# A new order of operations for a two-layer linear-attention and GLU kernel, searched with longer and more frequent delays of DMA transposes

The kernel runs on one core of one Trainium2 chip. The metric is the device time of one execution in microseconds (us), median over runs.

## The reference

Two layers, applied in turn twice (A, B, A, B) with the same weights, on x of shape (1, 2048, 512) in bf16.

```python
def _A_ref(x, wqkv, w_phi, wo):                  # 32 heads of 16
    q, k, v = ...                                # x @ wqkv, split
    pq = jnp.einsum("bhsd,hdf->bhsf", q, w_phi)
    pk = jnp.einsum("bhsd,hdf->bhsf", k, w_phi)
    phi_q = concatenate([softmax(pq), softmax(-pq)])     # phi_k likewise
    kv = jnp.einsum("bhsf,bhsd->bhfd", phi_k, v)
    z  = jnp.einsum("bhsf->bhf", phi_k)
    o = einsum(phi_q, kv) / (einsum(phi_q, z) + 1e-6)
    return o.reshape(B, S, D) @ wo

def _B_ref(x, W_gate, W_up, W_down):             # F = 1376
    return (relu(x @ W_gate) * (x @ W_up)) @ W_down

x = A_x
x = x + _A_ref(_layernorm(x), ...)
x = x + _B_ref(_layernorm(x), ...)
x = x + _A_ref(_layernorm(x), ...)
x = x + _B_ref(_layernorm(x), ...)
```

## The kernel before

The kernel records 2114 operations, each with its engine, its planned duration and what it reads and writes. A list scheduler then simulates the engines and takes, whenever an engine comes free, the ready operation of the highest priority. The priorities are a table of 2114 numbers (`RANKS`, packed as text), found by a search outside the kernel; `MOVED` lists operations that run on their second engine. After that each engine gets its own fixed stream with semaphore waits.

```python
    def schedule(self, rounds=12, ranks=None, moved=()):
        for i in moved:
            o = self.ops[i]
            o.eng, o.fn, o.ii, o.lat = o.alt
        self.links()
        if ranks is not None:
            self.boost = {}
            return self.forward([float(r) for r in ranks])
        # ... (priorities from the graph, if there is no table)

    def emit(self, e, eng, sems, dsems):
        for o in self.seq[e]:
            for s, c in o.waits:
                if isinstance(s, tuple):
                    eng.wait_ge(dsems[s[1]], 16 * c)
                else:
                    eng.wait_ge(sems[s], c)
            ins = o.fn(eng)
            # ... (the semaphore increment)
```

A token tile is 128 rows of x, and there are 16. The layer norm's result y of a tile is transposed before PE multiplies with it. Most tiles are transposed by a DMA that the SP engine issues (a few by PE itself); so are the q features, the attention output o and the remainder of the GLU's hidden values. That makes 99 DMA transposes, of 128 KB each for y.

```python
            if (l, t) in PE_Y:
                # ... PE transposes y into PSUM (line 655), ACT copies it out
            else:
                op("sp", lambda e, yt=yt, dst=dst, c=c:
                       e.dma_start_transpose(dst.ap()[:, :, c:c + 128], yt.ap()),
                   reads=[yr], writes=[rr], dma="tr", nbytes=500, name=f"yT{l}.{t}")   # line 660
# ...
        for b in range(2):
            op("sp", ... e.dma_start_transpose(...), dma="tr", name=f"qT{l}.{t}.{b}")     # line 767
# ...
            op("sp", lambda e: e.dma_start_transpose(oT_.ap(), ot_.ap()),
               reads=or_, writes=[oTr], dma="tr", nbytes=500, name=f"oT{l}.{t}")          # line 931
```

Names in the text: "yT of tile 13, layer 2" is the transpose of y of token tile 13 in the second A layer (the four layers are numbered 0 to 3). Lines: L587 and L606 fold w_phi into the weights at the start; L682 computes the K and Q features, L739 V, L754 Q in another layout, L786 the key-value sums, L837 and L901 the attention output, L936 the product with wo, L966 gate and up, L994 the GLU remainder, L1020 down; L646 is y, L655 a transpose of y on PE.

The softmax here doesn't subtract the row's maximum and nothing guards it: scores larger than these inputs give would overflow.

## Time and profile before

| | before |
|---|---|
| time, median of 3 runs | 385.53 us (385.19 to 386.15) |
| profiled run: span | 383.0 us |
| PE busy in it | 371.3 us, 97% |
| PE's idle time in it | 11.7 us |
| DMA transposes | 99, of which 18 landed 3.0 us or more after issue, the others 2.4 to 2.8 |

The busy row says that PE is the bound; the stretches say where it idles at all; PE's wait list says what for. The prediction below shows these views, line by line. A landing is the moment at which the data of a DMA are there, and "DMA to landing" counts from the issue.

### The profile page before, as it was taken

Reading aid. Unit: us, or ns where it says so; the run is one execution under the profiler, and the core shown is the slowest. Engines: PE = TensorE matmul, PEld = TensorE weight load, DVE = VectorE, ACT = ScalarE, POOL = GpSimd, SP = SyncE. Lnnn points to the kernel's source line nnn. Section 1 sums busy time; section 2 is a strip of 40 time slices with the busy share of each in tenths; the row PEclk is TensorE's granted clock in tenths of the full one; section 3 lists DMA queues with packets and bytes.
Section 4 is the critical chain, followed back from the end, with each engine's and each line's share of the span. In section 5 each row is a group of like instructions: output and inputs, shape, how many; then the busy total and the mean of one; then the engine's idle time right before and its main releaser. Section 6 shows DMA issues by size and latency. Waiting matters only on the chain.

```text
span 383.0 us, 6646 instructions
## 1 busy us (share of the span) xinstructions
PE 371.3 (97%) x2429; PEld 206.4 (54%) x2471; DVE 292.0 (76%) x646; ACT 199.7 (52%) x618; POOL 58.2 (15%) x123
## 2 busy tenths in 40 slices
...
DMA packets 64944, 23.94 MB, mean 63 GB/s; under 512 B 56112, under 2 KB 64656, under 8 KB 64912
## 3 DMA queue, kind: packets, MB, share of 16 engines
...
## 4 chain that ended last, share of the span: by engine, by line
PE 80%; DVE 10%; DMA 4%; ACT 2%; issue 2%; POOL 1%; SPq 0%
PE pb L966 36%; PE pb L1020 18%; PE pb L936 7%; PE pb L754 4%; PE pb L739 4%; PE pb L837 3%; PE pb L994 3%; DVE z L701 2%; DVE phik L708 2%; PE pb L1022 2%; PE pb L786 2%; DMA yT<-y 2%; PE pb L682 2%; DVE z L703 1%; DVE y L646 1%
## 5 line engine op out<-in xcount | busy, mean ns | idle before, releaser
L974 DVE TENSOR_TENSOR expq<-gate,pb 128x512 bf16<-128x512 bf16 (+1 forms) x100 | 57.1, 577 | 46.6 <-PE pb L966 46.3
L973 ACT ACTIVATE gate<-pb 128x512 bf16<-128x512 f32 (+1 forms) x100 | 50.8, 510 | 68.9 <-PE pb L966 64.7
L966 PE MATMUL pb<-yT,Wu 128*128 128x512 bf16 (+1 forms) x396 | 82.8, 336 | 0.3
L966 PE MATMUL pb<-yT,Wg 128*128 128x512 bf16 (+1 forms) x393 | 81.4, 336 | 0.4
L1020 PE MATMUL pb<-Wd,expq 128*128 128x512 bf16 (+2 forms) x320 | 75.4, 373 | 0.5
L966 PEld LDWEIGHTS pb<-yT,Wg 128*128 128x128 bf16 x400 | 38.3, 98 | 30.1 <-DMA yT<-y 0.4
L966 PEld LDWEIGHTS pb<-yT,Wu 128*128 128x128 bf16 x400 | 38.8, 98 | 28.9
L1020 PEld LDWEIGHTS pb<-Wd,expq 128*128 128x128 bf16 x330 | 31.6, 98 | 35.4 <-DVE expq L974 0.6
L620 DVE BATCH_NORM_STATS2 stats<-x_sb 128x6 f32<-128x512 bf16 x64 | 43.4, 686 | 1.0 <-DMA x_sb<-in_A_x_dram 0.5
L695 ACT ACTIVATE phik<-pb 128x512 bf16<-128x512 f32 x72 | 39.6, 639 | 1.2 <-PE pb L682 1.2
L1028 DVE TENSOR_TENSOR x_sb<-x_sb,pb 128x512 bf16<-128x512 bf16 (+2 forms) x33 | 21.9, 665 | 20.3 <-PE pb L1022 20.0
L629 ACT ACTIVATE lnv<-mv,eps 128x1 f32<-128x1 f32 (+1 forms) x58 | 16.8, 297 | 35.3 <-DVE mv L621 34.8
L700 POOL TENSOR_TENSOR t<-phik 128x512 f32<-128x512 bf16 x16 | 19.1, 1195 | 88.3 <-ACT phik L695 83.2
L758 ACT ACTIVATE expq<-pb 128x512 bf16<-128x512 f32 x56 | 30.7, 604 | 3.1 <-PE pb L754 2.9
L739 PE MATMUL pb<-wv,yT 128*128 128x512 bf16 x123 | 30.0, 380 | 1.6 <-DMA yT<-y 1.2
L936 PE MATMUL pb<-wo,oT 128*128 128x512 bf16 x120 | 30.9, 379 | 0.5
L874 DVE TENSOR_TENSOR t<-pb,sm 128x384 bf16<-128x384 f32 x56 | 29.4, 547 | 1.5 <-POOL sm L864 1.5
L682 PE MATMUL pb<-Wkp,yT 128*128 128x512 bf16 x124 | 29.6, 379 | 0.1
L646 DVE TENSOR_SCALAR y<-x_sb,mv,rstd 128x512 bf16<-128x512 bf16 x63 | 27.1, 439 | 2.3 <-ACT rstd L631 1.8
L851 ACT ACTIVATE sm<-pb 128x48 f32<-128x48 f32 (+1 forms) x84 | 14.4, 211 | 26.5 <-PE pb L837 26.4
L754 PE MATMUL pb<-yT,Wqp 128*128 128x512 bf16 x106 | 25.9, 380 | 0.4
L939 DVE TENSOR_TENSOR x_sb<-x_sb,pb 128x512 bf16<-128x512 bf16 x32 | 21.8, 683 | 3.4 <-PE pb L936 3.1
...
## 6 DMA issues: line engine op xcount, KB each, us to landing
...
yT<-y SPq DMA_TRANSPOSE x55, 2.5
...
```

The costliest lines, as they stand in the source:

```text
L620: op("dve", lambda e, t=t: e.bn_stats(stats[:, t, :], x_sb[:, t, :]), reads=[res("x", t)], writes=[res("st", t)], ii=600, lat=690, name=f" ...
L646: yop[l, t] = op("dve", lambda e, t=t, yt=yt: e.tensor_scalar(yt.ap(), x_sb[:, t, :], mv[:, t, 0:1], rstd[:, t, :], ALU.subtract, ALU.mult ...
L682: i = e.matmul(kt.ap(), src.ap()[:, ic, c0:c0 + 128], W[:, ic, :], start=(ic == 0), stop=(ic == 3))
L695: op("act", lambda e, s=s: e.activation(ft.ap()[:, :, s, :], kt.ap().rearrange("p (g f) -> p g f", f=64), ACT.Exp, scale=(1.0, -1.0)[s]), ...
L739: i = e.matmul(vt.ap(), src.ap()[:, ic, c0:c0 + 128], wv[:, ic, :], start=(ic == 0), stop=(ic == 3))
L754: i = e.matmul(qt.ap(), Wqp[:, ic, c * 128:(c + 1) * 128], src.ap()[:, ic, :], start=(ic == 0), stop=(ic == 3))
L758: op("act", lambda e, g=g: e.activation(es[g][0].ap(), qt.ap(), ACT.Exp, scale=(1.0, -1.0)[g]), reads=[qr], writes=[es[g][1]], ii=477, lat ...
L936: i = e.matmul(wt.ap(), oT_.ap()[:, c, :], wo[:, c, :], start=(c == 0), stop=(c == 3))
L966: i = e.matmul(pt.ap()[:, 0:n], W[:, ic, fc * 128:(fc + 1) * 128], src.ap()[:, ic, a * 128:b * 128], start=(ic == 0), stop=(ic == 3))
L973: op("act", lambda e: e.activation(st_.ap()[:, 0:n], gt.ap()[:, 0:n], ACT.Relu), reads=[gr], writes=[sr], ii=110 + n * .72, lat=230 + n * ...
L974: op("dve", lambda e: e.tensor_tensor(ht.ap()[:, a * 128:b * 128], st_.ap()[:, 0:n], ut.ap()[:, 0:n], ALU.mult), reads=[sr, ur], writes=[h ...
L1020: i = e.matmul(pt.ap()[:, 0:n1 - n0], hT[l, s, fc].ap()[:, c:c + 128], Wd[:, fc, n0:n1], start=(fc == 0), stop=False)
```

## The change

The search that found `RANKS` and `MOVED` draws noise on the durations of operations and prefers orders that stay fast under it. The new tables come from a search in which a DMA transpose was delayed more often and for longer. Code and operations are the same; the diff has only tables.

```diff
 RANKS = (
-    '9sqX)M*%<xF9<gXe*!)T-Uk8*!T_EG5eDW1I|w}pRs}x@*9O=J`~-LhNe46t1PB8NDhRIwB?t-#D+i(m$p;Sr$_HEr0ssL3Q3n733;;X`I|dE_0|2cB9S9!?',
     ... (all 45 lines of the table replaced)
+    'hX*1D^at(*Lk0~9^#{!dK?q$0vIVgRqz9=76bKLqAO#=>p9kLuzy~l09SE8S3J44cF9_=f90&yn>jioQF$kan82~;A7YH8!EC?e2HwYF80RRO6001)xApjNt',
 )
 MOVED = (
-    73, 75, 93, 101, 143, 245, 305, 325, 471, 472, 475, 481, 497, 547, 599, 627, 643, 644, 647, 651, 667, 692, 699, 715, 716, 740, 767, 771, 788, 791,
-    812, 1470, 1488, 1536, 1544, 1561, 1568, 1592, 1612, 1640, 1656, 1657, 1680, 1681, 1688, 1705, 1712, 1729, 1732, 1736, 1752, 1760, 1780, 1800,
+    73, 79, 87, 93, 101, 143, 245, 325, 471, 472, 475, 481, 490, 497, 498, 547, 579, 599, 620, 623, 627, 643, 644, 647, 651, 667, 675, 699, 716, 723,
+    739, 743, 747, 764, 812, 819, 835, 836, 839, 1470, 1536, 1537, 1544, 1568, 1592, 1609, 1616, 1633, 1636, 1640, 1656, 1684, 1688, 1705, 1708, 1712,
+    1732, 1736, 1756, 1760, 1777, 1801, 1804,
 )
```

More of the change, by code (lines that the diff above doesn't have):

```diff
@@ L1110 @@
 RANKS = (
-    '9sqX)M*%<xF9<gXe*!)T-Uk8*!T_EG5eDW1I|w}pRs}x@*9O=J`~-LhNe46t1PB8NDhRIwB?t-#D+i(m$p;Sr$_HEr0ssL3Q3n733;;X`I|dE_0|2cB9S9!?',
-    '7623g1ppTa1OSQ#90(Br3IMhRBM77bD+VM8%>|+X6#yIr2mqG_r3YFD4FD4W69|C^e+OIw2>>AoY5?g55eO{^4hUla1_9v%1^^}q5&+c%6bL>CTmUl&3jnbP',
-    '8VDi?3<#eGga=s$c>#z9;0Im?3kZ=1!~tdi76?rT^aVZ!IS4HSK?M~E5(w)D^anu*ya750L<a~6@dNS)HV7~X#Rs_uRR?te2LKreum|S{qzCQ?dk41%H3#Vj',
-    'A_Wf!vIpA-#|9z?p$0ApLI+a^DhJO8^9P0pm<I_6)CV94tq0Nv2ME0e`Ub)W1_=5GCkLAc&<9ip9taZ$kO#d7MF+D7{Ri9z1_#Cml?Q4ET?eKId<Sp`Xa)oa',
@@ L1115 @@
-    'x(CAs7zecm5(kb4@dkYd8V7s^<p%%<+y@{B&IZ2*uLnE@;RoFZ1_kB>UI(rRP6F=(F$muWWC!9083$DbwgPGfX9xBNTLxeT)dwsH*9Gqe=mo?FZU@u`ZwEIA',
-    '^#*VTF$ehu5CAm>8UQ&5z6PfUSqG~IT?PRL{st%q<OGHWHwCr_pazl#%?2d~U<c0w?geHCD+v1qV+XDVjt1uj?*$$QO9%S~2?rMk8wZmH9|zC{GY9bnH3<I(',
-    '*apl8G6<grqy|R@K?igOhX-Z`7X~;7BL|`fTL+#7>jtj|s0Tj>S_hd1$p-WWxCS-{atDA1P6q=AiwCC$wg$omQU{I&yasg!-UeR>CI^uQf(P~m<Ofj(xdw#>',
-    '%?BL^VF!-}NCyK3rUvl`od=2sGzTvS(+B7Vng&1z>IPW_+XfW}mIn|Ai3f`YL<Xz}!3MVmb_Wp$YX*!5o(Ba66bGCI$_9i6(FWuOAqU<C(guYGKn17<#0HN9',
@@ L1119 @@
-    '`~`ak8wP&{ng<O8>IJL?{RWW*vIY_cQw5a<N(b5ofdxGVJO+9OB?n&yMFtNAqXlvWj|Wc&*#m$C<^}`=^#|<+PX_!3p$FIl{RBJ&kpTz-f&{$-s{_;n+XHR|',
-    'tpsfav<6`YivzI%;|Ie7Uj@Ge-vc`Wa|OExTn5<(MhEx?zz2*3$Oh;K@CR21bO#6qa|Y%IzXt#adIdcNBL+AK!3QY_@&+gf{0Bn@_XpVqDF!VEss%#@{|B50',
-    'm<4MGg9n!eVg_Xd3j(SF90#oiCIuS^*aSxhPzUb^@dN<~5C!lBg#~y8d<16%Xa#x)Z3evr?E~utaRyxl;|6C2$po1NB?bEj)doxltN<qnItQf&aR=H5G6(Dj',
-    'qX(%61qg`-k_U|issySA%mzdS3I}KhkOmkC)(7|pxCi+M%Lo1k?FXv|&IhmtHwF+04G6;rc?MPoJO`ZyP6Z1FYzF-UPzI9+I|pnB-v-DB_695mn+6RAz6S>f',
@@ L1123 @@
-    '4F_Qa&IF(ba|8wk@&(ofy9Uz*1qXEpeg^>ut_9Ht;RXx_5(WMR_Xa2iX$O=C2nP%Ymk0R;CI<fn+67kxsRn!nF$D_+LkAuPas)63_5>XURRl~1%LWAnQ3bRI',
-    'hzE@a*9QUycLm%9)dkE1Z3is|-35UI5d|0q#|Hog@CG^ta|iAQeFiZGsRWG%6b8ly&<3Cd8U>*RN(EyD*#tTRW(1Z6+Xd$Z2L{*$wFhqo?gVEAR0e|vp9LBQ',
-    'HU?M+!v!P;-UN~bFa@s#SO(4oegqr^umrmW83qmpvjpY^4+ixGCj}J-zXgy5hy{BEhXttxG6uW_F$84>s|6tiYXs~BV+5N8QU$;U#Rbs?j0PqIlLYq!KL*VN',
-    '<pjb7hX#xVQv|vNw*_Mc9|oiZP6R3jZU$flUIlOk7X?WLxCH0~WCcY8@B^X*Zv+4ZWd~dZNd!Ixx&(Lx9tBth_XDW{IRj<|6a<zAtpno)N(RydAqEWveFTsM',
@@ L1127 @@
-    'lm^QM2?cisGX*OJ4+p&kIt9Q5MFWNf-vz@2B?P<#1O?Ou69lXTQUn<Vas%!I&jiW@)&%ebbOizjRtDt;5Ck0s!UVDfSp+WyY6N8kvjN-$wgf5!eg((`=mHu9',
-    'iUcDBVFgwMxdk}{;01vMTLdfwg9BOwPz09*LIxxS9|AH3%L6L}Tm)$ZrvyR-0|l4{vj(69?Ezi{5(FX!-2_(!s07;tN(3wh3<Z@1{RM&s(giRENCr6uY6Zy!',
-    'F9z%e?FF0$&jzdpyaz`Gcm@^+ss}v>3I=utc?T{Ax(4?J>Id@$1O|ZyQwEs_I0h#MMFmL)(+1rJ4hIVd$OWDSrUgL;Pz6W@#{@11<puZ!l?0Ooq6K6I(*!dH',
-    'P6kT`HUxwO`UMsS!37%yKn5HJT?8!!lm+4imIF)$qXrNL8UxG)vjxQlDFv_vng#y^I|R!FwFR98IR*Oz69v}<gavj5#{;tiLjr6AGXy^aa{~zkYXkZMxdX-o',
@@ L1131 @@
-    'bpwI}RRbOaUjt(U+yYz!>;(x1j|Hs)H3ilNBnKb_>I0tx{{v(L6$G#XbOXo&ZUU|YQU=`vI|FV6DFhb-`~xflxdKK7WCWZ8E&~??9Rzs=g9J?kq65wYy8|}^',
-    'Z3I{ZD+4nFssWe-G6A~)xC6BUlL3eVHUgXi9|27T1q8|iz6In3O9f2^djvHEpaXvcQUfXjO#|HmPy-SJsRJAXbOM$F(f}3%6a{tydjiD(qy@wUeg=XCPX#mu',
-    'm;_=4GzRGe3I*8(iUk7%jRcDYI|Z}^TLp3kfCkhA69%ybYXy1)e*}XCLIrsQBm|`e?F2>!rUWPjfCYaA^91h%uLN)e$_3{H2nFi|b_ARRE(9n9^#sKPJp*t9',
-    '=>?|+k^_DN(F17%0t5vE<N}HVg91wg>jU5fF9g~Go&);=kON)=nFBrpQv>V+00Zm-T?1JI1_Uq!_5=9@AO$!CR|eq(=mU8J*8?~MNdx@?%>p3<Bm;{Cg#_dS',
@@ L1135 @@
-    '4+J9vZv(CbngsF!)&q?L9|QFQPXm+#AOi*i?E;bnQ3QPju>_d}i3Onq;0Cw_KLvCI2L*8j&jkkrR0Z<}u?A@dbp@ye3j|sP^aJ|@76jo19|evCRR-Gvxdh_`',
-    'w*<xo!2}Eh;s$60s{|he#R3im-vkx~_yi{e5d_r(Ed<~Lh69NMz5-|iG6YHk3IoytM*~y>O9ABq5CfY8;{(kDbp+l6Oa!h1Z3CzSrUQ%v`~tuOcLPHM*8(L2',
-    '!~*yO+5@`;0t1=@{sXrHK?4~Bw*v?RvICO?S_4@E3<C`VNCO@O;saL$#RED7d;|IeR0CTB?gH-tq5@$9LIdXl;R0X-Yz34AP6KHLG6T#5n**N&ECsX$#|4%I',
-    'AO_F`)&j%?hy=O=cmqcS0tNI0qXbU`0R+<m2?PEFi3EoPAp{!)L<EZh&jKn1z68tyU<7dlA_PVRJ_Nu7vIO}983Yal(gWoKqXRz#+ymzWl>?OmKm$Aj*a9L0',
@@ L1139 @@
-    'gaTUv1Ow{=;sWyn(*r{U7zBm{X9IWwH3N|Y>H@z4lL8n64g(znu>(c}Jp{Z1E(O8^zXM+cL<0*0y#mGp`UF4%CIjFB8Ul<0{{kig$OE+lv;*J*Vgzmj$pR4r',
-    'O9M6o!veMgHU-K8Gz6Ce!2;?8)dIu=7zNG(kp!y(x&qMzBL&_8;sm__y8<)<4gr|}Isg{{o&gyEApoQSdI5m|6ajYudIFsR0|Ivkd;!V;Dgn&^Py+Y>uL95m',
-    '=>rM`2n1#Wk^(>kdjSCjZ34gn@&o_`z5`SQhy!m00|SBr8~_6W_5fA`odkpcgaMrc;{Xi;fdU=^umhz8JpoJuz5yu*Vh3pf@B&8wNCFuFK>|nw_yTeQ;{x*n',
-    '?*fSe8vrB##sdTb7y#`6Z~^ZCLIDQ?wFImKp#vZQY6IQ^fB{_sI0Z=oH3C)udjtLfhXZT`p#mNO;{hlE=>ib}G6FdQD*|2uI0B~w#sKgE(E{!OGy@m`d;+}z',
@@ L1143 @@
-    't^pweCjof^u>vpxYXIi~Q3I<1Q38zt76H@(AOUFtL;>yrfC32ug#vK^eFD`0g#)w#j|15Psss4~Y65oxiUKhMO#+qyD*;#l$N(t;Pyx3AR{~!EWdZ^LUjn5A',
-    '&;X7D%>my6gabDO@&oAs4g%x>LIM{8b_1^fqysPm6a#AlRs!V!fCE+mj{@2RC<2rMaRbW&W&$Sz@d4%nEdufZHv(D!J^|4Hp8}fz;sL?}69V}GQv$dGVFH^1',
-    'xB&nHmjVX^&jGOj6ao_iyaE;i*a1uerveuN$pD%GS^~KN{{j920s`v+{Q;i=YyvX?JOEMvumRrzaRMCzY5}hS&H--#A_8Lpn*s9xvI2|%`T=MF^Z}p&>;a|$',
-    'rT_{7dIL=WZvuJ%DFQ44&;tAb^8vL1_yKzW3jvA%4*}!=(g7v`#{n<_5CYKwNC5@{MgV^SYXLg|OaWd13<C85g#k+fhXOAHKLSAkR{>K2f&n)G$^k(Dm;!zR',
@@ L1147 @@
-    'F#$gT2LWIKZ2^M;kpR~LRRIM8SOPZzWdZa8=m5h2#{wt-Q~^2xPXRyyGXZ@8jsd9vN&z7OoB<~Qask!=qXN$WF9B}>lmK7=QvfLdSpXUVtpO?kqXD!5Jp!iy',
-    'tN|MXDFed+mH<)#r2*9e906MaVF6|V4FPom^Z-f#wgHC$0Re6R@Bl~vE&)yewgB+}HUXRfmjGt~Yyf@%KmbDkzyOE<m;lEBWdJPzVE`onX98ma!2>=53Id7&',
-    '`v9{7@d82s<^e$jWdi{N9{{WZqyiNMQUZ<wjRG|Q5CK&Jzye<ZN&-&;VgmO9R{%2tM*_(ME&?S2BLY|hi2)G;kOHOxMFJH9+yO-ZIsz&J4+Gi(VgO(Q^#kew',
-    'AOcAOkpeLSeFNwLJOV8N83OwOodVMVq5#wZ`~kuNh5-@+Z~|}uh5(2G7y^p{cmcWrXaY|F-2uh{y8){JX#gk#&;cX@Cj$2Yp#iu6h630Ck^tZUo&XX7{Q!6X',
@@ L1151 @@
-    'jsWEWVguU&sR5M%-T*`b90GF!LjgYkr2_T=nE`GAlmXcRi2&IEngUn>`T(Z^T>(u2a{(&=XaSi5_5v>g6$4}faRF=r0RqVZMFC;~H39bkP65*Z4+81{umDB@',
-    'v;YVJxd4X%Gy$#vmjROivH(N?bOBxgBmuVoI{{q)b^*)*wE&C(asVs=O8}?>;Q{La+yFQMkO7?l1OdMRo&q!gfdT&jz5r1HfB+o<A^~&&bpV(Fr~obiG5}ct',
-    'r2wq}qX60f>;RAeBLUU{paS^-WC7OzTmg#!PyjvvTL3Wt)BwK#OaK)D9RS||jR1oHg#fw$H~`B4IRKRaBLFr4vj8RlZ2(jN+W?>d%K_&AB?0~b$N@$IvH=?c',
-    'k^u|>p#a4J;Q&zpe*l62j{z(IX93~>!2$IE%m6$AS^=5>!2o^$@&LR5!~g&R=>VSqssITAr~!5WRRD7U69MJ`-2gcONdSBRcK~Dn8v%I$JpeBN&H#@9A^-&e',
@@ L1155 @@
-    'eE={3',
+    'hX*1D^at(*Lk0~9^#{!dK?q$0vIVgRqz9=76bKLqAO#=>p9kLuzy~l09SE8S3J44cF9_=f90&yn>jioQF$kan82~;A7YH8!EC?e2HwYF80RRO6001)xApjNt',
+    '5da1N4geDX7XTapA^;TtKnVW^5C8%I1OPt>+XZU^B>*G{2>=NM2LLz-3jhNE5(qX2CkO)wJqQ^H4FK^68VD)~9sv6X8vq;uG6>fN!2$395&$9y6aXLy%mEk(',
+    'JP4Nu8Ue@$+Xw6h4*)I(`3BnrGzi27WdsfguLm9o1PC1fiUwu}1_&|)@CP9X7yzpWyamYzs0Z=|tOgnYP6kp3Z3i?5<_C@k2?&)1Q3q)Ug$H5>>j%sR)&}hd',
+    '=La7L7zg|Z$pZ)oHwT*s_y^?$GzJj}?gsz}NC$BSkO##F0to&Grw4ooO$8eWeFuIAMh653k_S)+2MA;bYX{&5o(4S!bO%-k=?1(8eg<|2ItO_N3I@{$xCej+',
@@ new lines @@
+    'i3idLTL<q4BnN^9We4X5QwKf=#s>-q$OcUZy#~$%<p&rA)(7?nUj`Betq0==X$2(+lLr0-mIk*6ssxk<DF`bFZ~`d+fdy3tBM96FzXwYO6$i8j3IKKnya%@i',
+    '90#HX3kabGI|xz*oCZJ!nFmA#^ac+IoCh@qItU#BkObERA_bKP_62+e3<XsL2mnO|3;^K=&j*MHCI}!0?gjw|rUp3&JO?KS@C6VDF9*2?U<cs_+6GhwLkEEd',
+    'ItDlg7YDlsDhA#K{RKP)T?ftuGX~oRMh4slK?aZprv{M+zXnGKum>Rr2?tdNatD|P&<3Rk69;<-Fb9_g0|(^>I0eE7p9bRvK?hL-ZwK=RB?iC-u?5Zss0J$r',
+    'MF+tK00+?qg9i@>U<GamI|tbYH3!!Ro(C!iG6!Y`83(}!Q3i(wP6tc}od=x;cLvx8%LaV~#|AD3iwCd<X9w~I`~`9b{RUnI-v%QFN(R>kKnDW`nFdJ))Cb)I',
@@ new lines @@
+    'cLZq$-vvho-353B{|Ed8V+LRbbp`hYBLuPp_y$%5Y6c7ktOqCrfdu9Q=LNO|$p*&*vIlAb7Xp?8YXjc{tOQ5}kOeaYbOBNT2?Fc~-2!d_EC2)p?gUu{d;p#V',
+    'D+dGyXa*++djRqW0SLwen*@^p3Iw?UdIo_9vj(*X)d%(lH3*0XVF!f-u?A-bn+8?}_Xj@&wg-&|{s!~~<OVqi)ds=_R0oC!ods71-Um?yGyseS*$3(d`Ul+y',
+    'V+S7yz6Q((dI!P;z6Bu$d<K69k_Hn9M*uAaYzG|#Y6pb|=mx0<z6aw14F`7zln0Lolm(>$t_4H~$OT>oeE}N>>I0((kp@x*lLzPrlmx>B9tSoCB?TV^76*L>',
+    'rU$hKcn4Ys=?4}DSqDr8IR*m-m<Id?C<T@WjRva*+6VmyfCm%@J_9uXh6N)BaR(>|p$BjWTm+2;qXk?CbOuZWIsmW%{{>zLga<ta>IWSL$_5e#MFxxn0s^`Q',
@@ new lines @@
+    'm<7QF#Rba;%?1Sqd;~fL%LUd2pa(k!SOZT7EC)6S^9Q{L;s>q=VFAhq`3Lm|wg%A$LI*nqumt-BWCSn;y9CMvvj^Y?iv}D9<Oc=^83t$vNeAHtSO;?i(go%Q',
+    'kp*i8a0aIZpasAM83pD9pac^I{{$8VJp>d6hy*MKa|c-l&<AV=l?I9jZ3MUmga)Vug9fPuLIjQlc?K&5c?E|9ngu2Y5(N$hCj~(T#|H@p!UdNF`32Mlx(9;=',
+    'J_Zj48wSAxeFRViVFbDbqz2Xm9t7D1y#>DoDFyEZx&-$InFWjm9tL&-;|2x>e+GI5^aQm9xCAl=Km_6jv;_$T=L6FQh6Zp2K?7F?2L&1jKLvLMjs!debOp}@',
+    'R|Wk9umv&&VFuy_B?qMiDF;Rcl>}o2-3A>6R|7ExZUi(1rvv^4>ICNmc?6FJmIOEiUj&H-83Zl`o&_=kfCTje*#YSSjRQ*svIhDFQv+KD4FnMeWCl(I!~_)v',
@@ new lines @@
+    'qXxqUZ3W;300aUBss;K5mjwI*f&%~s?FQup@&a20eFJ3%rvhaKXa(E_h67*(RRx>{gawfV7Y20(hXn@*I0p9wbq9$C{sZ;|#{{PY%L8f!%>t|g6b1JKe*~BW',
+    'j{_+Kp9B*GL<S}V8w1w^j0Xq=UIEkqS_5_jzXaq1*amY3O$3Pqf&~f#vjnOG8w3~z0|OQWUIR}AT?GvT(*+y_g9O3@t^)!FKL<|*(FMZ?HU;1WQwHw_-Ujdn',
+    '=>>uZOaNR3@dk?pNd&qAF$NU~UkB*~2L>nzJq2zCE(oy%N(WB{xdt}|ss~*L3<k{w#0Sm?0tYP!%LIf3qy=^b&jxJ<Aq5KsGY1+5n+0M9Zw40y*aZy+Rs*;N',
+    '=mq8lBn2n~$pwxEiUg|zBnDar4g|CYWCc714h0SeR0cu@m;(z2IR#h-$OKLWg#~H^VgnNfq6JU}(gw-}tp?r%!v!z~IRuacS_LWvCI!0#?gRY;LjxrQp#zx#',
@@ new lines @@
+    '8Uj894+NV7QUllnWda5S#|3)@(*#}w8U<MdxdmSZt^{=h+6DRp69W|kXamLqNCb)lo&vxG;RGWE2nCq~VFSJbF#;?FH3aGfZv>JA+ysjRq6C@)g9Et)wFA`x',
+    '#05_RGy^yTKm&gRLI73(&H^F>gaVWT#R232hX6AL)dQpihy~9Ay#u=j1O(^<g#$(e<OK%<>jU2cZv*%Qj01lHssc6yMgZLb*Z~Uy_5!c~Yz2}7p8_`pYy@Ei',
+    'r3Ntv3kMws0R}Y%Tm~ux1qa3kuLDa23I%2b2nU%2Zw0mmiUlGDKL&CI)C5TdSOo+HVg-o<%mvv5Qw0wLF9rYwQUo;vss=3wTLd=*9|nd59|Y<FCI&VGw*(~v',
+    'odlo;bOSj9W&^(iX#<=B4g(Mak^(~n;RC}1(gUIg)dh0}wgSKdegkj>Faz}hlLhAj`vUR=F$4z$5eKXV&;{TFp#=K`?*n`T4+R1Q?E)SJMF4sOCIk5bX$0H@',
```

21 lines of the change are left out of this document (added).

## The prediction

> **What bounds the kernel now.** I read first the page's busy row and 40 slices, then the stretches of time, then PE's own wait list, then PE's timeline around each wait, and last the landing times of the DMA transposes.
>
> The page:
>
> ```profile
> PE 371.3 (97%) x2429; PEld 206.4 (54%) x2471; DVE 292.0 (76%) x646; ACT 199.7 (52%) x618; POOL 58.2 (15%) x123
> ...
> PE 80%; DVE 10%; DMA 4%; ACT 2%; issue 2%; POOL 1%; SPq 0%
> ```
>
> PE is busy 97% and holds 80% of the chain that ended last. The change reorders work and moves none to or from PE, so it can win at most what PE idles: 383.0 - 371.3 = 11.7 us. Of that, 20.00 - 17.58 = 2.4 us lies in the first 20 us and 43.00 - 40.43 = 2.6 us in the last 43 (nearly all in the last store). The stretches, whose columns are window, length, and busy time of PE, PEld, DVE, ACT and POOL:
>
> ```profile
> 0.00:20.00 20.00, 17.58 (x149) 12.53 (x152) 17.65 (x61) 15.88 (x41) 7.19 (x33) 1.00 0.62 192
> 20.00:40.00 20.00, 19.86 (x94) 9.03 (x95) 19.80 (x38) 19.57 (x59) 13.79 (x18) 1.00 0.55 120
> ...
> 128.00:200.00 72.00, 71.68 (x354) 33.95 (x358) 46.21 (x99) 23.46 (x67) 2.06 (x4) 1.00 0.16 31
> 200.00:215.00 15.00, 13.67 (x62) 6.07 (x63) 15.00 (x21) 13.82 (x37) 1.16 (x1) 1.00 0.40 78
> ...
> 340.00:383.00 43.00, 40.43 (x205) 19.59 (x207) 16.84 (x27) 6.63 (x12) 0.00 (x0) 1.00 0.13 40
> ```
>
> From 128 to 200 us PE idles 0.3 us in 72, so that third has nothing to give. Where DVE is full too (20 to 40, 200 to 215), a late DVE step delays PE. PE's waits, by line and releaser (total us, times, longest):
>
> ```profile
> PE pb L739 <- DMA yT<-y: 1.2, 1, 1.2
> ...
> PE pb L994 <- issue: 1.0, 1, 1.0
> PE pb L606 <- ACT yT L477: 0.9, 1, 0.9
> PE pb L655 <- ACT sm L863: 0.7, 1, 0.7
> PE pb L655 <- DVE y L646: 0.6, 1, 0.6
> PE pb L786 <- DVE phik L708: 0.5, 1, 0.5
> PE pb L901 <- DMA expq<-phik: 0.4, 1, 0.4
> ```
>
> These seven, 1.2+1.0+0.9+0.7+0.6+0.5+0.4 = 5.3 us, are what an order could win. In PE's timeline they stand at 211.77 (L739), 80.18 (L994), 18.82 (L606), 250.97 and 67.07 (L655), 44.67 (L786) and 243.58 (L901). Now the transposes, as the yT tile's view and the chain of waits give them:
>
> ```profile
> DMA to landing us min/median/max: 2.4/2.5/4.6
> ```
> ```profile
> 207.69 4.03 DMA yT<-y
> ...
> 239.10 4.43 DMA expq<-phik
> ```
>
> Going through the issue and landing of all 99 DMA transposes, 81 land 2.4 to 2.8 us after issue and 18 take 3.0 to 4.6. Three of those 18 stopped PE: the one issued at 75.48 (4.60 us; it is the wait called "issue" at L994, since PE starts 0.09 us after the landing), the one at 207.69 (4.03) and the one at 239.10 (4.43). Together 1.0+1.2+0.4 = 2.6 us. That is the loss that the change aims at.
>
> [...] 15 matmuls of 512 columns took 3.24 us from 219.93 in the chain, 216 ns each, although their mean recorded duration is 380 ns. [...] so I take 216 ns. [...] SP's record of a transpose is 1.27 us, its landing 2.5 us. [...] a y of 0.40 us takes three for 1.89 us at 27.93 while a POOL addition runs.
>
> **The change part by part.** Only the priorities and the list of moved operations differ, so the same 2114 operations run, in another order; PE's matmuls are the same in number and shape.
>
> Moved between engines. Five more of the final additions o leave DVE (17 on POOL against 12): 5 x 0.42 = -2.1 us of DVE, +5 x 1.16 = +5.8 us of POOL (58.2 before, so free). Four more small products and sums come to DVE (35 against 31), +4 x 0.2 = +0.8. Of the PSUM copies one WkT, one WqT, one v and one oT leave DVE and one yT comes, about -0.42 -0.42 -0.68 -0.42 +0.42 = -1.5; one BD goes to POOL, -0.3. DVE: -3.1 us of 292. ACT gains three copies net at 0.6 recorded, 0.48 in a row: +1.4 us. Off the bound except in the DVE-full stretches. There, before 45 us, DVE loses 0.68 + 0.42 = 1.1 us.
>
> Transposes. For each I summed, in the two built orders, the PE work between the last PE instruction that must be done before the transpose can be issued[...] and its first reader on PE, at 216 ns per 512 columns. Of 99, those with under 6 us fall from 24 to 15, under 5 us from 8 to 6; the smallest stays 3.9. A chain through one DVE operation and an undisturbed transpose needs some 0.2 + 0.5 + 2.5 = 3.2 us, a delayed one up to 5.3. So the new order buys what it claims. Wait by wait:
> - 80.18, 1.0 us: before, the y of token tile 3 was ready at 74.48 but SP issued tile 2's transpose first, so it left at 75.48. Afterwards tile 2's y is two DVE operations earlier and its transpose goes before an oT. Leaving at about 74.5 with PE arriving at about 79, even 4.6 us would cost only 0.2. Gain 0.8.
> - 211.77, 1.2 us: y of tile 13 loses three DVE operations ahead of it (two reductions of 1.2, one of 0.67), and one 1.27 us issue ahead of it on SP, but its matmul comes 2.3 us earlier too. Just before it PE must now transpose tile 15 itself, whose y stands behind some 5.1 us of DVE work counted from y of tile 13 (0.4+1.2+0.7+0.5+1.2+0.7+0.4). By these it is ready near 209.0 with PE there near 208.1, a new wait of 0.9 in place of 1.2. Gain 0.3.
> - 243.58, 0.4 us: the work ahead of this reader goes from 8.4 to 13.5 us. Gain 0.4.
> - 18.82, 0.9 us: the two WqT copies on ACT stand behind the copy of V0.3 and no longer behind two exponentials of K0.2. ACT is full, so about half: gain 0.5.
> - 44.67, 0.5 us: DVE's normalisations come 1.1 us sooner and the sums are spread among the V and Q matmuls. Gain 0.4.
> - 67.07 and 250.97, 1.3 us together: both keep the same order (y waits for the x addition just ahead, PE has 0.2 to 0.5 us of other work). Gain 0.
> Sum -0.8 -0.3 -0.4 -0.5 -0.4 = -2.4 us.
> New exposure: the transpose of tile 13 in the last layer falls from 18.6 to 4.75 us of work ahead of its reader, others stay at 4.8. Undisturbed they fit; with 18 of 99 delayed I allow +0.5. Net -1.9 us.
>
> **The rivals.**
> (a) Whack-a-mole: the delays fall at other transposes or hit as hard. For it: three of 18 delays stopped PE, and the new order still has 15 transposes under 6 us. Against it: fewer are close. It would leave 385 to 386.
> (b) DVE is the real bound where PE waits (20.00 to 50, 200 to 215), so that more room for transposes changes nothing and only the 1.1 us taken off DVE counts. For it: DVE 19.80 of 20 and 15.00 of 15. Against it: between 75 and 80 us the wait was a landing, and three waits ended on DMA. It gives about 384.5.
> (c) Robustness is paid for: work done earlier for transposes displaces other work, moved o take 1.16 us instead of 0.42 in a chain, and small new waits on DVE and ACT appear. For it: tile 15 above. It gives 386.5 to 387.5.
> (d) All seven waits vanish: 380.2.
>
> **Range and chances.** 385.53 - 1.9 = 383.6. The three timed runs before span 385.19 to 386.15, 1.0 us, so the sum is about twice the noise. Range 381.5 to 386.0, from most of (d) to (a). Faster by 2% would need 7.7 us, more than all seven waits together; slower by 2% would need as much new idle time. Chances: faster 0.02, same 0.96, slower 0.02.
>
> **What would show it.** PE busy stays near 371. The wait of L994 on a landing near 79 us falls under 0.3; that of L739 near 210 is replaced by L655 on DVE's y, near 0.9; L901 on expq is gone; L606 on ACT is near half; the two other L655 waits of 0.6 and 0.7 stay. The share of transposes over 3 us stays near 18 in 99, but their first readers come later. It is wrong if PE's idle sum does not fall by about 2 us, if a landing stops PE again by over 1 us, or if PE's idle time grows in the stretch from 128 to 200 us, where nothing was to be won.

The sum comes to -2.4 us, with +0.5 for new exposure to -1.9 us net. The durations in it are those in the trace of before: o 0.42 us on DVE (L883) and 1.16 on POOL (L884), small products and sums 0.18 to 0.22 (L858, L860, L864), PSUM copies on DVE 0.42 and 0.68 (L478), BD 0.28 (L574), y 0.41 (L646), reductions 1.20 (L703) and 0.67 (L701). In the chain of 3.2 us the 2.5 is the median landing; 0.5 for a DVE operation and 0.2 ahead of it are estimates (y takes 0.41 us, and a matmul of 512 columns is recorded for 0.38 us where the next starts after 0.216). For a late DVE step that delays PE, the chain that ended last has hardly anything but DVE steps from 34.8 to 44.6 us, ahead of PE's wait of 0.52 at 44.67, and from 199.9 to 207.7 us, ahead of yT and PE's wait of 1.22 at 211.77. The three y of 1.89 us at 27.93 are two of 0.41 and one of 1.25; beside that one POOL's addition runs for 1.31 us from 28.36.

## The result

| | before | changed |
|---|---|---|
| first job, median | 385.40 us (4 runs) | 384.75 us (4 runs) |
| copy, 5 rounds, median | 385.9 us (11 runs) | 384.1 us (6 runs) |
| third copy, 5 rounds, median | 385.79 us (11 runs) | 384.05 us (5 runs) |

Ratios here are the mean time of one kernel's runs over the mean of the other's in the same rounds, so they are not quite the ratio of these medians. They are 0.9975 (95% interval 0.9958 to 0.9993), 0.9951 (0.9935 to 0.9968) and 0.9959 (0.9945 to 0.9972). The change gains some 0.25 to 0.5%, 0.7 to 1.9 us: within the prediction's range and far below 2%. All outputs are right. Kernels are compared only within the same rounds.

The page of the changed kernel, busy row and the chain that ended last:

```profile
PE 372.9 (97%) x2471; PEld 205.6 (54%) x2471; DVE 289.7 (76%) x641; ACT 201.1 (53%) x621; POOL 63.5 (17%) x125
...
PE 71%; DVE 21%; ACT 3%; DMA 3%; issue 1%; SPq 1%; POOL 0%; DVEq 0%
```

DVE fell by 2.3 us, ACT rose by 1.4, POOL by 5.3, against -3.1, +1.4 and +5.8 predicted. PE's busy time rose with the number of matmul records (2471 against 2429, with 2471 weight loads in both): it is the same work with more of its records kept. So PE's idle time of a page can only be compared between traces with equally many records. The chain now has 21% of DVE instead of 10%: at some places where a landing used to be the last to arrive, a DVE operation or PE itself is now. The stretches (window, length, busy time of PE, PEld, DVE, ACT and POOL):

```profile
0.00:20.00 20.00, 16.13 (x150) 11.07 (x150) 15.77 (x57) 15.73 (x41) 7.28 (x32) 1.00 0.62 192
20.00:40.00 20.00, 19.20 (x94) 8.57 (x91) 19.90 (x37) 19.12 (x56) 11.31 (x17) 1.00 0.45 100
128.00:200.00 72.00, 72.00 (x361) 34.24 (x360) 46.04 (x102) 23.54 (x66) 2.14 (x5) 1.00 0.16 31
200.00:215.00 15.00, 15.00 (x74) 6.94 (x73) 14.97 (x23) 14.38 (x39) 2.19 (x2) 1.00 0.49 79
```

Between 200 and 215 us PE no longer idles (15.00, before 13.67). In the first 40 us it idles 4.7 us, before 2.6. The gain and a loss therefore lie in different places. PE's waits in the changed kernel:

```profile
PE pb L587 <- DMA Wd<-in_A_wqkv_dram: 1.4, 1, 1.4
...
PE pb L739 <- ACT yT L477: 0.9, 1, 0.9
PE pb L682 <- DMA yT<-y: 0.8, 1, 0.8
PE pb L655 <- ACT sm L851: 0.7, 1, 0.7
PE pb L655 <- DVE y L646: 0.6, 1, 0.6
PE pb L786 <- DVE phik L708: 0.6, 2, 0.4
PE pb L994 <- DVE mv L621: 0.5, 1, 0.5
PE pb L606 <- ACT yT L477: 0.3, 1, 0.3
```

L739 waiting for a DMA (1.2) and L901 (0.4) are gone, and L994 fell from 1.0 to 0.5. The two waits of L655 stayed. Two are new, both near the start: L739 for an ACT copy (0.9) and L682 for a DMA (0.8).

### A table of lost time

To put numbers on stages I took, for chosen PE operations, the start in the trace minus the planned PE durations of everything ahead of them in PE's stream (216 ns for 512 columns, as measured: 15 in 3.24 us from 219.93 in the trace of before). This is PE time lost so far, and it allows two different orders to be compared. From the traces of two runs of the kernel before and three of the changed one, the loss within each stage, in us:

| stage (first operation to first operation) | before | changed | means differ by |
|---|---|---|---|
| start to the WqT transposes (near 10 us) | 4.06, 5.31 | 5.15, 4.83, 4.72 | chance of the start, see below |
| to the first R, L837 (near 52) | 2.91, 2.77 | 3.61, 3.61, 3.82 | +0.84 |
| to the first gate matmul (near 69) | 1.53, 1.54 | 1.89, 1.90, 1.89 | +0.36 |
| to the first Q of layer 2 (near 197) | 1.19, 1.65 | 0.51, 0.10, 0.24 | -1.14 |
| to V of tile 8, layer 2 (near 222) | 1.37, 1.62 | -0.02, -0.02, -0.03 | -1.52 |
| to R of tile 4, layer 2 (near 247) | 0.79, 0.59 | 0.79, 0.79, 0.80 | +0.10 |
| to the last down matmul (near 379) | 0.89, 0.91 | 0.75, 0.74, 0.74 | -0.16 |

Without the start the sum is -1.5 us. After the first stage the runs of one program agree within 0.5 us, in half of the cases within 0.1; the first stage differs by up to 1.25 us between two runs of one program.

### The profile page after: what moved, and what is told of

It is laid out like the page before. It is cut to its first block, busy times and chain, and to the rows that moved or that the text cites. A ratio compares the mean times of both kernels' runs of the same rounds, so it can differ in the third digit from the quotient of the medians.

```text
span 382.9 us, 6682 instructions
## 1 busy us (share of the span) xinstructions
PE 372.9 (97%) x2471; PEld 205.6 (54%) x2471; DVE 289.7 (76%) x641; ACT 201.1 (53%) x621; POOL 63.5 (17%) x125
## 4 chain that ended last, share of the span: by engine, by line
PE 71%; DVE 21%; ACT 3%; DMA 3%; issue 1%; SPq 1%; POOL 0%; DVEq 0%
PE pb L966 36%; PE pb L1020 18%; PE pb L936 6%; DVE z L703 5%; DVE phik L708 5%; PE pb L837 3%; PE pb L994 3%; DVE stats L620 2%; DVE z L701 2%; DVE y L646 2%; PE pb L1022 2%; DMA Wd<-in_A_wqkv_dram 2%; PE pb L754 1%; DVE rz L720 1%; ACT phik L695 1%; DVE x_sb L939 1%
## 5 line engine op out<-in xcount | busy, mean ns | idle before, releaser
L1020 PE MATMUL pb<-Wd,expq 128*128 128x512 bf16 (+2 forms) x330 | 76.9, 372 | 0.0
L700 POOL TENSOR_TENSOR t<-phik 128x512 f32<-128x512 bf16 x16 | 20.1, 1263 | 99.3 <-ACT phik L695 93.8
L936 PE MATMUL pb<-wo,oT 128*128 128x512 bf16 x128 | 32.4, 379 | 0.0
L739 PE MATMUL pb<-wv,yT 128*128 128x512 bf16 x128 | 30.6, 379 | 0.9 <-ACT yT L477 0.9
L682 PE MATMUL pb<-Wkp,yT 128*128 128x512 bf16 x124 | 29.7, 379 | 0.8 <-DMA yT<-y 0.8
L646 DVE TENSOR_SCALAR y<-x_sb,mv,rstd 128x512 bf16<-128x512 bf16 x63 | 27.6, 444 | 2.1 <-ACT rstd L631 2.0
L754 PE MATMUL pb<-yT,Wqp 128*128 128x512 bf16 x112 | 27.2, 379 | 0.3
L884 POOL TENSOR_TENSOR o<-t 128x512 bf16<-128x512 bf16 x17 | 19.7, 1158 | 39.1 <-DVE t L874 29.3
```

What stands on the lines that cost most here:

```text
L646: yop[l, t] = op("dve", lambda e, t=t, yt=yt: e.tensor_scalar(yt.ap(), x_sb[:, t, :], mv[:, t, 0:1], rstd[:, t, :], ALU.subtract, ALU.mult ...
L682: i = e.matmul(kt.ap(), src.ap()[:, ic, c0:c0 + 128], W[:, ic, :], start=(ic == 0), stop=(ic == 3))
L739: i = e.matmul(vt.ap(), src.ap()[:, ic, c0:c0 + 128], wv[:, ic, :], start=(ic == 0), stop=(ic == 3))
L754: i = e.matmul(qt.ap(), Wqp[:, ic, c * 128:(c + 1) * 128], src.ap()[:, ic, :], start=(ic == 0), stop=(ic == 3))
L936: i = e.matmul(wt.ap(), oT_.ap()[:, c, :], wo[:, c, :], start=(c == 0), stop=(c == 3))
L1020: i = e.matmul(pt.ap()[:, 0:n1 - n0], hT[l, s, fc].ap()[:, c:c + 128], Wd[:, fc, n0:n1], start=(fc == 0), stop=False)
```

## The experiments

### Copies of both kernels

No edit. The first profiled pair had equal spans (383.0 and 382.9 us) although the timed runs differed, so I ran both word for word again.

> A copy of the kernel before, the control: ratio 1.000 within 0.001. Wq columns: theory A 8.9 to 10.1 us, theory B near 8.9. Late transposes: the same 17 or 18 places if they belong to the program, among them those issued near 75.5, 207.7 and 239.1 us; other places if random.

> A copy of the changed kernel, for what differs from run to run. In the first traces the load of the Wq columns, issued at 3.16 us in both kernels, landed at 8.91 us before and at 10.10 after, and PE waited 1.4 us for it after. Theory A (that landing is luck of the run): it lands between 8.9 and 10.1 here, and PE's wait at the transposes of Wq changes with it, 0 to 1.4 us. Theory B (something in the new order makes it late): 10.0 to 10.2 again. For the transposes: if their long landings (15 of 99 over 3.0 us) belong to fixed places of the program, the same ones are late again, above all the y of tile 3 of the first GLU layer (4.6 us in both first traces); if they are random, at most a fifth of them are the same. Time 384 to 385, ratio to before 0.9975 within 0.002.

Measured: copy of before 385.94 us (ratio 0.999, interval 0.9971 to 1.0009, span 384.6), copy of the changed kernel 384.1 us (ratio 0.9951, just outside the forecast of 0.9955 to 0.9995; span 382.2). The first profiled run of before had simply been lucky: its load of the Wq columns landed at 8.91 us, and in every other profiled run of the first six at 9.78 to 10.33, and PE waits for it. That it is luck and not the order shows in a later run that begins with the new order (the second splice below): there it landed at 8.83. The copy's wait list shows it, and shows the old waits in a run with an ordinary start:

```profile
PE pb L739 <- DMA yT<-y: 1.6, 2, 1.5
PE pb L994 <- issue: 1.4, 1, 1.4
PE pb L587 <- DMA Wd<-in_A_wqkv_dram: 1.4, 1, 1.4
```

L587 <- Wd is the wait for Wq, 1.4 us; it stands in the changed kernel's list above as well, and the prediction's wait list of the lucky run has no such line. It has nothing to do with the change.

More important is that the copy of before had late transposes (3.0 us or more) almost exactly where the first run had: 16 of the first run's 18 were late in it again (the other two took 2.8 and 2.9 us), and 15 of the changed kernel's 16 in its copy. If delays were drawn at random for each transpose, as the search's noise is, 18 of 99 would hardly fall on the same ones twice. So I looked for what else was moving data at these moments. The trace's packets have a kind "instruction", which I read as fetches of the engines' own programs. Of packets of 16 KB there are 19 or 20 in a run. Between two of them PE has 252 instruction records on average in the first run of before and 254 in that of the changed kernel (126 to 358), so I read them as PE's. Packets of 8 KB, 17 to 20 in a run (13 of 19 within the span in each of these two), come on another queue (q14). In the first run of before 17 of the 18 late transposes overlapped an instruction packet in time. Here is the DMA view of the copy of before from 211.0 to 213.0 us (40 slices of 0.05 us: busy tenths, then GB/s; then the queues with packets, MB and share of 16 engines):

```profile
DMA  9994910000006000000000003779999999899760
GB/s 230 195 215 113 380 21 0 0 0 0 0 0 164 0 0 0 0 0 0 0 0 0 0 20 67 164 169 220 195 241 225 215 205 210 174 184 143 82 46 5
...
q8 instruction: 1, 0.02, 3.6%
q14 instruction: 1, 0.01, 1.7%
```

A transpose is running at about 200 GB/s. At 211.2 us a 16 KB instruction packet comes (the 380), at 211.6 an 8 KB one (the 164). Then nothing moves until 212.15, and the transposes go on. The 16 KB packet holds one of the 16 engines for 1.2 us (3.6% of 16 x 2 us). In PE's timeline of the same run (start, duration, engine, line, idle time before it and its releaser) the price stands directly:

```profile
213.59 0.60 PE L739 MATMUL pb<-wv,yT 128*128 128x512 bf16 x2 [1.46 <-DMA yT<-y]
```

yT of tile 13, layer 2, left at 209.28 and landed at 213.55, 4.27 us later. In the copy of the changed kernel it left at 205.35, landed at 207.90 (2.54 us) and PE used it at 208.77 without waiting:

```profile
205.35 1.27 SPq L660 DMA_TRANSPOSE yT<-y  x1
```
```profile
208.77 1.03 PE L739 MATMUL pb<-wv,yT 128*128 128x512 bf16 x4
```

The fetch lay at 209.5 us there, behind the landing. It delayed tile 14 instead (4.15 us), which had 10 us of slack.

Over all 14 profiled runs 218 transposes took over 3.0 us (up to 5.0), and 211 of them overlapped an instruction packet. Of the 1168 others 184 did (16%). Counted the other way: of 237 transposes that overlapped a 16 KB packet 166 were late, of 158 that overlapped only an 8 KB packet 45, of 991 that overlapped neither 7. So an overlap does not always make a transpose late, but almost none is late without one.

### Moving PE's program by 128 instructions

If fetches delay transposes, they must move when PE's program is moved against its work. I added waits that are already fulfilled ahead of some early PE operations. Two of them make one instruction (the traces have 128 more records for these 256 waits), so this is 128 instructions, half of the 252 that lie between two 16 KB packets on average:

```diff
     def emit(self, e, eng, sems, dsems):
-        for o in self.seq[e]:
+        for k, o in enumerate(self.seq[e]):
+            if e == "pe" and 60 <= k < 92:
+                for _ in range(8):
+                    eng.wait_ge(sems["pool"], 1)
```

In both kernels everything else is the same, and so is the order.

> The order before with 128 more instructions in PE's own stream, waits that are long satisfied, spread over 32 matmul groups of the first layer[...]. In the traces so far 17 of the 18 late transposes of before overlap a fetch of instructions (16 KB packets near 76.5, 209.6, 241.0 us). Fetch theory: the late transposes move to new places, between the old fetches; those issued near 75.5, 207.7 and 239.1 land in under 2.9 us[...], and PE's waits for them, 1.0, 1.2 and 0.4 us, fall below 0.3 each; other transposes become late at the same rate, some 12 to 18. Time between -2.6 us (383.0) and +1 us (386.4), by whom the fetches now hit. Rival (random, or tied to the transfers in flight): the same places are late as in the copy, or places without relation to the fetches, time unchanged within 0.5 us.

> The same 128 instructions in the new order. In the trace after, 14 of 15 late transposes overlap a fetch. Fetch theory: y of tile 3 of the first GLU layer (4.6 us) lands in 2.4 to 2.6 us and PE's wait for it, 0.5 us, goes; the others move. As the new order has more work ahead of its transposes' readers, its time should move less than that of before: within 0.7 us of 384.75. If it moves as much as before does, the room it has is no protection.

Measured: before with the shift 384.78 us (383.18 to 386.10; ratio to before 0.9969, interval 0.9941 to 0.9997), the changed kernel with the shift 385.49 us (0.999, 0.9974 to 1.0007). The set of late transposes changed: the shifted before has only 9 (12 to 18 were forecast), and 5 of them are new. The 4 that stayed all overlap an 8 KB packet of the other queue. In the shifted before yT of tile 3 (layer 1), yT of tile 13 (layer 2) and qT of tile 2 (layer 2), the three that stop PE in before, were all on time, and from 52 us on its wait list has no wait for a yT at all (in kernels with added waits line numbers are higher by 3):

```profile
PE pb L658 <- ACT sm L866: 0.7, 1, 0.7
PE pb L658 <- DVE y L649: 0.5, 1, 0.5
PE pb L939 <- DMA oT<-o: 0.3, 1, 0.3
```

Its loss from the first R to the end was 3.56 us, against 5.77 and 6.31 for the unshifted before and 3.92, 3.51 and 3.64 for the changed kernel. So the old order, fetched at other moments, loses as little there as the new one. The changed kernel lost 4.15 us from R on with the shift, about 0.5 more than without, by waits of L939 of 1.0 us in sum, 0.6 of them for oT. Its time missed the forecast (within 0.7 of 384.75) by little, but against the copy in the same rounds it became 1.4 us slower, while the order of before became 1.2 us faster. By the expectation's own measure the room of the new order was no protection there, though some 0.9 of the 1.4 us lie ahead of R in the two traces. What the shift gained before it lost in part at the start: the added instructions stand where DVE and PE are both full (27.80 and 26.74 of 28 us between 11 and 39 us in before), and in the profiled run of the shifted before PE's matmuls of 128 columns also took 107 ns instead of 56 up to 13.9 us (granted clock of the whole run 0.996), for a loss of 10.5 us up to R instead of 7.0 to 8.1.

What follows: lateness goes with the place of the instruction fetch, and not with the transpose or with chance alone.

### Splicing the two orders

Priorities and moved operations of one kernel for the first 700 operations (all up to about the first attention outputs, 62 us), those of the other for the rest.

```diff
 RANKS = (first[:700] + second[700:])       # packed again
 MOVED = ([i for i in first if i < 700] + [i for i in second if i >= 700])
```

> Ranks and moved operations of the kernel before for the first 700 operations (the projections, the key-value sums and the first half of the first attention outputs), those of the changed kernel for the rest. PE then runs in the old order up to its 151st step (about 62 us) and in the new order from its 213th on. If the gain lies behind the first 60 us and the new order gives some back at the start, as the two profiled pairs suggest, this beats both: PE's lost time 6.5 to 8.1 us up to the first R step as in the kernel before, then 3.3 to 4.0 as in the changed one, so 383.0 to 383.8 us, 2.2 to 2.9 below the kernel before. If the gain needs the new order from the start (the rival), it stays at 384.5 or above.

> The reverse splice: the changed kernel's first 700 operations, the old rest. If parts add up: lost time of 8.4 to 8.8 us up to the first R step, then 5.0 to 6.3 (tile 13's transpose in layer 2, issued near 207 us, late again and PE waiting 1.2 to 1.6 us for it; the wait for tile 3's transpose near 80 us small), so 385.3 to 386.5 us: the kernel before within 0.7. If the start is where the change wins, as my prediction had it for 0.9 us, it comes out at 384.5 or below.

Measured, 5 rounds each on one chip: old start with new rest 383.84 us (ratio 0.996, interval 0.9944 to 0.9977), new start with old rest 385.36 us (0.9994, 0.998 to 1.0007), before 385.56. Both times came out as the adding up of parts says (the first 0.04 above its range); the second one's loss up to R was 7.7 us and not 8.4 to 8.8, because of its early Wq load. In the second one tile 13's transpose was late again, 4.12 us, and PE's longest wait is the old one:

```profile
PE pb L739 <- DMA yT<-y: 1.3, 1, 1.3
```

From the WqT transposes to the first R the two splices lost 3.06 (old start) and 3.82 us (new start), as the programs they come from (2.8 to 2.9 and 3.6 to 3.8). So the new order pays some 0.8 us in the first 50 us, and all it gains lies behind.

### Moving the fetches with the start left alone

Two more shifts, by the same edit at PE steps that come after the first R: 160 instructions in the order of before, 32 in the new order, there aimed so that a fetch should meet tile 13's transpose too.

```diff
-            if e == "pe" and 60 <= k < 92:
+            if e == "pe" and 120 <= k < 160:      # order of before
+            if e == "pe" and 140 <= k < 148:      # new order
```

> The order of before with 160 more PE instructions (waits that are already fulfilled) among its steps 120 to 159, near 56 to 74 us[...]. Shifting the measured fetch points by 160 instructions on the trace of the copy of before, only 4 of the transposes issued after 65 us would meet one (o of tile 9, layer 0; the GLU remainder of slab 2; o of tile 2 in layer 2; y of tile 10 in layer 3), against 12 without the shift, and none of the three that stop PE. Fetch theory: at most 6 transposes over 3.0 us after 75 us, the waits of 1.2 to 1.6 us near 80 and 211 us and of 0.4 near 243 us gone, a loss after the first R step of 3.0 to 4.0 us plus what 160 waits cost where they stand (at most 1 us), time 383.0 to 385.0. If the old order itself is to blame (too little room), the two big waits stay and it is 385.5 or above.

> The changed order with 32 more PE instructions among its steps 140 to 147, near 66 to 69 us. Shifted by 32, the fetch points of the copy of the changed kernel meet 10 of the transposes issued after 65 us, and among them that of tile 13 in layer 2, whose first reader comes only 0.9 us after an undelayed landing. Fetch theory: that transpose takes over 3.8 us and PE waits 0.6 to 1.3 us for it near 211 us, just as in the kernel before; the wait near 80 us goes to 0.1 or less; time 384.3 to 385.3, at most 0.9 above the changed kernel. If the new order is robust by its room, no wait for a transpose over 0.3 us appears near 211 us and the time stays at 384.1 within 0.3.

Measured: 387.42 us (ratio 1.0054, interval 1.0029 to 1.0079) and 385.57 us (1.0002, 0.9985 to 1.0019). Both forecasts failed in part.

In before with 160 the three known waits are gone as forecast (yT of tile 13 in 2.54 us, qT of tile 2 in 2.49, yT of tile 3 in 2.49). But 11 transposes after 75 us were late, not at most 6, one of them yT of tile 13 in layer 1, 4.04 us, with a new wait of PE near 146 us:

```profile
PE pb L997 <- DMA yT<-y: 0.9, 1, 0.9
```

And the added instructions themselves were not nearly free: between the first R and the first gate matmul the loss was 3.86 us instead of 1.54. That is 2.3 us for 160 instructions where I had allowed 1, so this run's time says nothing on the order.

In the changed kernel with 32 tile 13's transpose stayed on time (2.55 us). Its fetch had not moved: it came at 210.0 us, without the shift at 209.5 to 210.7. The fetches at 77.1, 90.9 and 268.6 us had moved, by 1.2 to 2.7 us (from 78.3, 93.6 and 270.4). So the place of a fetch is not simply a count of instructions; I can move fetches but not aim them. The one at 268.6 hit another transpose of the new order, oT of tile 7 in layer 2, which then took 4.14 us (266.47 to 270.62) instead of 2.5 and had 0.7 us of slack:

```profile
270.75 1.02 PE L939 MATMUL pb<-wo,oT 128*128 128x512 bf16 x4 [0.94 <-DVE mv L624]
```

The view names a DVE operation, but PE starts 0.13 us after the landing; it is the wait for the transpose. The kernel lost 5.2 us from R on, 1.5 more than without the shift. Of this 0.8 us was lost before the first gate matmul (2.65 us in that stage instead of 1.89), where the 32 instructions stand, so I count it as their cost. The 0.94 us are a late transpose: the new order, too, can be hit.

### A late and sparse shift for both

To get rid of the cost: 40 instructions, one ahead of each of PE's steps 270 to 309 (140 to 175 us), where PE only multiplies (busy 34.84 of these 35 us in before).

```diff
+            if e == "pe" and 270 <= k < 310:
+                for _ in range(2):
+                    eng.wait_ge(sems["pool"], 1)
```

> The order of before with 40 more PE instructions (fulfilled waits), one ahead of each of PE's steps 270 to 309, some 140 to 175 us, where PE is bound by its matmuls. Everything up to there stays as it is. The fetch of PE's instructions that met tile 13's transpose of layer 2 (at 211.2 us in the copy of before) comes 20 weight loads earlier, near 208.3, where only two q transposes with 31 us of room are in flight. Fetch theory: tile 13's transpose lands within 2.6 us, PE's wait of 1.2 to 1.6 us for it falls under 0.3, other waits for transposes stay within 0.5 in sum, and if the 40 waits cost under 0.5 us the time is 384.2 to 385.0, about 1.0 to 1.5 below the kernel before. If the old order's lack of room is to blame, the wait stays over 1.0 and the time is 385.5 to 386.3.

> The changed order with the same 40 PE instructions at the same steps. Here the fetch that lies at 209.5 us, behind tile 13's landing, comes to about 206.6, into its transposing (issue 205.4, landing 207.9, first reader at 208.8). Fetch theory: tile 13's transpose takes 3.8 to 4.4 us and PE waits 0.6 to 1.2 for it; time 384.7 to 385.6, that is 0.6 to 1.5 above the changed kernel of the same rounds, and not better than the order of before with the same insertion by more than 0.7. If the new order is robust by its room, it stays within 0.4 of the changed kernel.

Measured: before 384.96 us (six runs, one of them 387.38; ratio 0.9994, interval 0.9971 to 1.0017), changed 385.22 us (384.50 to 387.51; 0.9999, 0.9974 to 1.0025). The timing can't tell them from before: three of the changed kernel's six runs were slower than 385.7, two of them with a granted clock of 0.997 and 0.999. The traces can. The 40 instructions cost next to nothing where they stand (0.15 us between 137 and 197 us).

In before the fetch moved to 207.04 us, and tile 13's transpose took 2.53 us. But PE still waited 0.57 us, twice what I had allowed. SP's own timeline shows why (start, duration of the issue):

```profile
207.19 2.13 SPq L770 DMA_TRANSPOSE expq<-phik  x1
209.36 1.27 SPq L663 DMA_TRANSPOSE yT<-y  x1
```
```profile
206.99 0.40 DVE L649 TENSOR_SCALAR y<-x_sb,mv,rstd 128x512 bf16<-128x512 bf16 x1
```
```profile
211.94 0.60 PE L742 MATMUL pb<-wv,yT 128*128 128x512 bf16 x2 [0.57 <-DMA yT<-y]
```

Tile 13's y was ready at 207.39. SP had just begun to issue a q transpose, and that issue, under the fetch, took 2.13 us instead of 1.27. So y of tile 13 left 0.86 us later. At fetches the issue of a transpose is long too, and not its landing alone: issues of over 1.6 us (up to 2.6), next to a median of 1.2 us, are in every run, 3 to 7 of 99, and all 68 of them in the 14 traces met an instruction packet within 1.3 us of their start. In the new order tile 13's transpose is issued ahead of this q transpose. That is room that the order really gives.

In the changed kernel the aimed hit failed again (fetch at 210.2 us, tile 13 in 2.55 us); oT of tile 7 took 3.52 us and the loss from R on was 4.34 us, 0.7 more than in the plain copy.

### Old start with new rest against the changed kernel

The splice again, beside the changed kernel on one chip, both as above.

> The splice with the old start and the new rest once more, word for word, beside the changed kernel on one chip, to see whether it beats it. By the first run of the splice its start loses 0.7 to 0.9 us less between the first WqT transposes and the first R step, and its rest 0.3 to 0.6 more: 383.4 to 384.2 us, 0 to 0.6 below the changed kernel, which five rounds can just resolve or not.

> The changed kernel word for word, as the measure of the other three: 384.0 to 384.6 us, ratio to the kernel before 0.995 to 0.998.

Measured: 383.84 us (383.18 to 384.35; ratio 0.9952, interval 0.9937 to 0.9966) and 384.05 us (383.91 to 384.23; 0.9959, 0.9945 to 0.9972). Both as expected. The splice beats the kernel before by 0.5%; over the changed kernel its 0.2 us is not resolved. From the WqT transposes to the first R it loses 2.67 us against 3.82, but up to the WqT transposes 5.22 against 4.72 in these two runs. From R on it loses 4.25 against 3.64. It loses more around 80 us (1.2 against 0.2 us between the first gate matmul and layer 2), where in its order yT of tile 2 is late (4.38 us).

## Why the prediction was right, and where not

The time is right: 383.6 predicted, 384.05 to 384.75 measured, a gain of 1.9 predicted and 0.7 to 1.9 measured. The parts of the sum are less so; their errors cancel, which is luck.

- **80 us, -0.8.** Right. The wait fell from 1.0 and 1.4 us (two runs) to 0.1 to 0.5 (three), and by the kind of reason given: the transpose still took 4.2 to 4.6 us (before 4.6 and 5.0), but left earlier against PE. In absolute time it left at 76.3 to 76.6 us, later than before, and not at the 74.5 that I had worked out.
- **211 us, -0.3.** The mis-sized term. It is worth -1.5 (1.37 and 1.62 to zero). The step that failed is "a new wait of 0.9 in place of 1.2": y of tile 15 was there 0.35 us before PE, in place of 0.9 behind it. The 5.1 us of DVE work behind y of tile 13 took 4.6 (204.34 to 208.92), because I had added recorded durations that overlap (in before an L708 of 0.68 us starts at 204.44 and the next operation at 205.04), and PE came 4.9 us after the start of this work, in place of 4.2 (209.0 - 5.1 = 203.9, to 208.1). Also, I had counted that the same transposes would be late wherever they went; this one came off the fetch altogether.
- **243 us, -0.4.** Right for the wait, not for the stage: L901's wait is gone, 0.2 to 0.4 us, but the table's loss from 222 to 247 us rose by 0.10, because the new order loses 0.26 us at the first L901 matmul and 0.23 at a PE transpose of o of tile 0.
- **18 and 45 us, -0.9 together.** Wrong in sign. L606's wait for ACT fell from 0.9 to 0.3 as said, but a wait of 0.9 for an ACT copy came at L739 and one of 0.8 for yT of tile 6 at L682, which in this order overlaps an instruction packet of 8 KB (at 21.48 us) and takes 3.15 us. L786's 0.5 became 0.6 in two pieces. The stage loses 0.84 us more. The step that failed is taking half of each small wait as a gain where PE, DVE and ACT are full at once: here the wait that was removed came back at other operations of the stretch.
- **67 and 251 us, 0.** Right: 0.6 and 0.7 us stayed.
- **New exposure, +0.5.** The amount is near, the place is not. The transpose that I had named, yT of tile 13 in layer 3, landed in 2.45 us in all three runs. Of the +0.36 between R and the first gate matmul some 0.2 stands at a late transpose (oT of tile 3, layer 0, 3.04 us); the rest I can't assign. That this term came near is luck too.

Of the three signs that I had named for being wrong, two did not come: no transpose stopped PE by over 1 us in the changed kernel (0.8 at most; the landing of the Wq load did, by 1.4, which the copies show to be luck of the run), and between 128 and 200 us PE did not idle. The third, PE's idle sum, must be read from pages with 2429 records: 11.7 us (with the lucky load) and 14.0 before, 11.6 and 11.4 changed. So it fell by some 2.5 us against an ordinary run and hardly against the lucky one. The 11.7 us were also too large a bound: with all 2471 records the changed run has 10.0 us of idle time, so part of such a sum, by these pages at least 1.4 us (an estimate), is unrecorded matmuls.

Of the rivals, (b), that DVE is the bound, falls: between 200 and 215 us DVE is as full as before (14.97 of 15.00) and PE idles no more. (c), paid robustness, holds for the first 50 us, 0.8 us. (a), whack-a-mole, is half right: the gain at 80 us came by room, with the transpose as late as before, but that at 211 us, the largest of the table, came with a fetch that fell elsewhere, which no part of the prediction had foreseen. What my prediction took for delays that fall on 18 of 99 transposes and must be outrun with room lie where instruction packets are fetched (211 of 218), most of them at the 16 KB ones that I read as PE's (166 of the 211 late overlaps). From the first R to the end the order of before loses 5.8 to 6.3 us with its own fetches, 3.6 with the program shifted by 128, 5.3 with the late 40 and 7.3 with 160 (2.3 of it the cost of the added instructions). The new order loses 3.5 to 3.9 with its own, 4.2, 4.3 and 5.2 (0.8 of it such a cost) with shifts of 128, 40 and 32. So the old order alone ranges over 2.7 us, and the two orders with their own fetches differ by 2.3. In the stage of tile 13 (to V of tile 8) the old order, which lost 1.4 and 1.6 us with its own fetches, lost -0.01, -0.02 and 0.73 us with the shifts of 128, 160 and 40. That the fetches account for the late transposes and that an order can lose or win 1.5 us at tile 13 by them is shown. The new order does give room in places (tile 3, qT of tile 2 with 6.2 us of slack instead of none, tile 13's issue ahead of a q transpose). That it is the more robust one on average is not shown by these figures: without the cost of the added instructions they are 5.8 to 6.3, 3.6, 5.3 and 5.0 for the old order, 3.5 to 3.9, 4.2, 4.3 and 4.4 for the new one.

Left open: what decides the exact moment of a fetch (two aimed hits missed), and what within the DMA engines keeps a transpose waiting while a packet of instructions occupies one of them.
